# Attention with two expert layers: the same instructions, with tiles at other byte addresses modulo 256

## The chip, the cores and the metric

The kernel runs on one core of a Trainium2 chip. The metric is device time in microseconds, of which the median of the runs is quoted. One run was taken with the hardware profiler, and every row below comes from that one. "Address" means the byte offset of a tile within each of the 128 partitions of the on-chip memory (SBUF); a "residue" is that address modulo 256.

## The reference, cut to what matters

```python
keep = is_sink | in_window                       # 4 sinks, window of 128
a = softmax(where(keep, q @ k.T / 8, -1e9))
x = (a @ v) as [1536, 512]                       # 2 batches x 768 tokens, 8 heads x 64
h = x @ w_in                                     # [512, 2048]
g = where(h >= 1, h, where(h <= -1, 0, (h + 1) ** 2 / 4))
x = g @ w_out                                    # [2048, 512]
h = x @ w2_in
g = where(h > 0, h, exp(min(h, 0)) - 1)
out = g @ w2_out                                 # [1536, 512]
```

All four weights arrive as 64-bit floats.

## The kernel before, in words

The 1536 tokens are three blocks of 512. Attention (class `Attn`) makes the input of the first expert layer and the two layers (class `Moe`) follow; attention's pieces for later blocks are put between the first layer's products by hand (`between`, `PULLS`).

A product of two 32-bit numbers is made of three products in the faster type fp32r: each operand is split into a high part and a remainder (hi and lo), and hi·hi, hi·lo and lo·hi are added up. So an activation block t has two tiles, `xh` and `xl`, each [128, 4, 512]. A step ("item") is one block of tokens with one slice of 128 hidden units. `wsplit` (L148 on) makes four weight tiles of [128, 512] for it: ScalarE casts the high parts, `wh0` and `wh1` (L158), and GpSimd subtracts the remainders, `wl0` and `wl1` (L160; VectorE does the first sixteen items). 0 is the slice of the layer's first matrix, 1 of its second, and each of the four has two buffers. `gemm1` does 12 matmuls of 512 columns (L171): the weight tile is the stationary operand, loaded in pieces of 128 columns, and `xh` or `xl` is the moving one. Then the gate is computed (ScalarE and VectorE), and the gated part is split in turn into `gh` and `gl` (L187, L188; three buffers each). `gemm2`, two items later, does another 12 (L210): in the first layer the weights are stationary and `gh`, `gl` move, in the second the gated parts are stationary and the weights move. `finish` (L267) is the same for the last two items. This is 96 items and 2304 matmuls of 128 by 128 by 512.

Each matmul has a weight load of its own (LDWEIGHTS). The load for the next matmul runs while the present one streams its moving operand, so that two tiles are read from SBUF at the same time: the moving operand of matmul n and the stationary operand of matmul n+1. Every slice that a matmul takes starts a multiple of 512 bytes into its tile, so a tile has one residue for all its slices.

The pools lay tiles one after another. Constants come first (10 KB from address 16384), then `x`, then attention's pools, then the experts'. Their sizes happen to be such that every tile of the experts begins at residue 160 before the change. Attention's are spread: `idn`, the identity for transposes (L466, L539), at 192; `P`, the probabilities, in four buffers at 96, 128, 160 and 192, of which the first to be transposed in a pair of heads is that at 96 or at 160 in turn; `one` at 96, `vs` at 160, and `pst`, their moving operand (L597 and L601, fp32r, 256 columns), at 224.

Of the kernel before, what the change touches and what calls it, by code (L numbers as in the profile page):

```python
# [7 lines left out]
F32 = mybir.dt.float32  # L8
F32R = mybir.dt.float32r
# [10 lines left out]
BLK = 128  # L20
KW = BLK + NSINK
WP = KW + BLK
NEG = -1.0e30
FILL = -1.0e9


def f32(ap):
    return ap.bitcast(F32)


def read_params(nc, const, n_sink, window):
# [33 lines left out]
class Moe:  # L65
# [82 lines left out]
    def wsplit(self, i, e):  # L148

        if i >= len(self.items):  # L150
            return
        nc = self.nc
        m, tb, f = self.items[i]
        src = self.F[m, f][:, e * 512:(e + 1) * 512]
        pool = (self.ws_p, self.wo_p)[e]
        hi = pool.tile([128, 512], F32R, tag=f"wh{e}", name=f"wh{e}")
        lo = pool.tile([128, 512], F32R, tag=f"wl{e}", name=f"wl{e}")
        nc.scalar.copy(hi, src)  # L158

        (nc.vector if i < self.KF else nc.gpsimd).tensor_tensor(out=lo, in0=src, in1=f32(hi), op=ALU.subtract)  # L160
        self.spl[i, e] = (hi, lo)

    def gemm1(self, i):
        nc = self.nc
        m, (t, c0, n), f = self.items[i]
        hi, lo = self.spl.pop((i, 0))
        xh, xl = self.xts[t]
        h = self.h_ps.tile([128, n], F32, tag="h", name="h")
        for k in range(self.KD):
            for p, (w, x) in enumerate(((hi, xh), (hi, xl), (lo, xh))):  # L170
                nc.tensor.matmul(h, lhsT=w[:, k * 128:(k + 1) * 128], rhs=x[:, k, c0:c0 + n],  # L171
                                 start=(k == 0 and p == 0), stop=(k == self.KD - 1 and p == 2))
            if k == 1:
                yield
        g = self.t_p.tile([128, n], F32, tag="g", name="g")
        if m == 0:

            nc.scalar.activation(g, h, AF.Relu, bias=self.half, scale=0.5)
            nc.scalar.activation(g, g, AF.Square)  # L179
            nc.vector.scalar_tensor_tensor(out=g, in0=h, scalar=1.0, in1=g, op0=ALU.max, op1=ALU.min)  # L180
        else:
            nc.scalar.activation(g, h, AF.Relu, scale=-1.0)
            nc.scalar.activation(g, g, AF.Exp, scale=-1.0)  # L183
            nc.vector.scalar_tensor_tensor(out=g, in0=g, scalar=-1.0, in1=h, op0=ALU.add, op1=ALU.max)  # L184
        gh = self.g_p.tile([128, n], F32R, tag="gh", name="gh")
        gl = self.g_p.tile([128, n], F32R, tag="gl", name="gl")
        ac = nc.scalar.copy(gh, g)  # L187
        dv = nc.vector.tensor_tensor(out=gl, in0=g, in1=f32(gh), op=ALU.subtract)  # L188
        self.own = (ac.ins, dv.ins)
        self.g[i] = (gh, gl)  # L190
        yield
# [90 lines left out]
class Attn:  # L282


    def __init__(self, tc, ctx, q, k, v, xts, idn, const, segs, nq=2):
        self.tc, self.nc = tc, tc.nc
        nc = self.nc
        self.q, self.k, self.v, self.xts = q, k, v, xts
        self.B, self.H, self.S, self.D = q.shape
        self.scale = 1.0 / float(self.D) ** 0.5  # L290
        self.idn, self.const = idn, const
        self.nq = nq
        pool = lambda n, b, **kw: ctx.enter_context(tc.tile_pool(name="a_" + n, bufs=b, **kw))
        self.ld_p = pool("ld", 3)
        self.qk_p = pool("qk", 2)
        self.p_p = pool("p", 4)
        self.pt_p = pool("pt", 2)
        self.xb_p = pool("xb", 1)
        self.s_p = pool("s", 2)
        self.ps = pool("ps", 2, space=PSUM)  # L300
        self.sk, self.kept = {}, {}
        self.turn, self.spare = 0, []
        self.nat = {}
        self.first = None
        self.jobs = [(s, pr) for s in segs for pr in range(self.H // 2)]
        for what in "kq":
            self.load(what, *self.jobs[0])
# [8 lines left out]
    def masks(self, prm):  # L316
# [4 lines left out]
        for j in (1, 0):  # L321
# [5 lines left out]
                                  for ty in range(3)]  # L327
        new, sink, old = slice(KW, WP), slice(BLK, KW), slice(0, BLK)

# [375 lines left out]
@with_exitstack  # L705
def attention_moe_moe(ctx, tc, q, k, v, n_sink, window, w_in, w_out, w2_in, w2_out, out):
    nc = tc.nc
    B, H, S, D = q.shape
    NT, DM = out.shape
    const = ctx.enter_context(tc.tile_pool(name="const", bufs=1))  # L710
    xp = ctx.enter_context(tc.tile_pool(name="x", bufs=1))
    ws = ((w_in, w_out), (w2_in, w2_out))

    raw = read_params(nc, const, n_sink, window)
    half = const.tile([128, 1], F32, tag="half", name="half")
    nc.vector.memset(half, 0.5)
    idn = const.tile([128, 128], F32, tag="idn", name="idn")
    nc.gpsimd.memset(idn, 0.0)
    nc.gpsimd.affine_select(out=idn, in_=idn, pattern=[[-1, 128]], compare_op=ALU.not_equal, fill=1.0, base=0,
                            channel_multiplier=1)  # L720
    NX = NT // 512
    xts = []
    for t in range(NX):
        xts.append((xp.tile([128, DM // 128, 512], F32R, tag=f"xh{t}", name=f"xh{t}"),
                    xp.tile([128, DM // 128, 512], F32R, tag=f"xl{t}", name=f"xl{t}")))
    full = [(t, 0, 512) for t in range(NX)]

    with ExitStack() as c2:
        NQ = 2
        segs = []  # L730
        for b in range(B):
            for q0 in range(0, S // BLK, NQ):
                tok = b * S + q0 * BLK
                segs.append((b, q0, tok // 512, tok % 512))
        attn = Attn(tc, c2, q, k, v, xts, idn, const, segs, nq=NQ)
        moe = Moe(tc, c2, ws, out, xts, (full, full), half)

        attn.load("q", *attn.jobs[1])
        attn.load_vsink()
        warm = const.tile([128, 1], F32, tag="warm", name="warm")  # L740
        nc.scalar.activation(warm, half, AF.Exp)

        zero = moe.t_p.tile([128, 512], F32, tag="g", name="zero")
        nc.vector.memset(zero, 0.0)
        bank = moe.h_ps.tile([128, 512], F32, tag="h", name="warmup")
        for _ in range(3):
            nc.tensor.matmul(bank, lhsT=zero[:, 0:128], rhs=zero, start=True, stop=True)
        prm = params(nc, const, raw)
        attn.masks(prm)
        gen = attn.stages()  # L750
        done = [0]

        def go(n=None, upto=None):

            while done[0] < len(segs) and (n is None or n > 0) and (upto is None or done[0] < upto):
                if next(gen) is not None:
                    done[0] += 1
                n = None if n is None else n - 1

        need = [(t * 512 + c0 + n) // (NQ * BLK) for t, c0, n in full] + [0]  # L760
        attn.spare = [lambda shape, name, t=t: moe.y_ps.tile(shape, F32, tag=t, name=name) for t in ("y0", "y1", "y2", "y3")]
        attn.spare += [lambda shape, name: moe.h_ps.tile(shape, F32, tag="h", name=name)] * 2

        for what, j in (("k", 1), ("k", 2), ("q", 2), ("v", 0)):
            attn.load(what, *attn.jobs[j])
        with tc.manual_schedule(engines={mybir.EngineType.PE}):
            go(n=1)
            moe.load(1)
            attn.load("v", *attn.jobs[1])
            moe.load(3)  # L770
            go(n=19)
        flag = windowed(tc, const, prm)
        with tc.manual_schedule(engines={mybir.EngineType.PE}):
            go(upto=need[0])
        moe.behind = attn.first
        attn.spare = []
        credit = [0.0]

        def between(i):
            m, tb, f = moe.items[i]  # L780
            if m == 1 or done[0] >= len(segs):
                return
            j = i // moe.KF
            credit[0] += PULLS[j]
            while credit[0] >= 1.0:
                credit[0] -= 1.0
                if done[0] < len(segs):
                    go(n=1)
            if f == moe.KF - 1 and moe.last_call:
                go(upto=need[j + 1])  # L790

        moe.run(between)

    cond = nc.values_load(flag[0:1, 0:1], min_val=0, max_val=1)
    with tc.If(cond < 1):
        with ExitStack() as c3:
            general_attention(tc, c3, q, k, v, prm, idn, half, xts)
        with ExitStack() as c3:
            moe = Moe(tc, c3, ws, out, xts, (full, full), half, pfx="g_")
            moe.run(lambda i: None)  # L800
# [32 lines left out]
```

## Time and profile before

| | |
|---|---|
| median of 3 runs | 661.54 us (661.34 to 661.99) |
| the profiled execution | 662.93 us, of which 661.2 us from its first to its last instruction |
| TensorE, matmuls | 638.8 us busy (97%), 3090 instructions |
| TensorE, weight loads | 500.5 us (76%), beside the matmuls |
| ScalarE / VectorE / GpSimd | 450.6 (68%) / 376.2 (57%) / 267.8 us (40%) |
| mean granted clock of TensorE | 0.991 of full |

How to read it: a matmul is pipelined, and its record lasts longer (389 ns and more) than the time until the next one starts. So the busy share of TensorE says that it hardly ever stood idle, and not how fast it went. How fast it went is read from start to start. The timeline gives starts to 10 ns; the chain of waits gives the length of a dozen in a row. Where a time from start to start stands below to 1 ns, it is taken from the trace's start times, which are kept in whole nanoseconds.

### The profile page before, as it was taken

How to read it: one execution, taken by the hardware profiler on the slowest of the kernel's cores; microseconds unless marked ns; L12 is line 12 of the kernel's file. 1: busy time of each engine (PE TensorE's matmuls, PEld its weight loads, DVE VectorE, ACT ScalarE, POOL GpSimd, SP SyncE). 2: the span in 40 equal slices, each digit the busy share in tenths (PEclk: the TensorE clock that was granted, in tenths of full speed). 3: DMA queues.
4: the chain of work that ended last, by engine and by line, in shares of the span. 5: the costliest groups of instructions: out<-in, count | busy, mean ns of one | idle time of the engine just before them, and what ended most of it. 6: DMA issues, size and time to landing. Idle time of an engine off the chain costs nothing.

```text
span 661.2 us, 9257 instructions
## 1 busy us (share of the span) xinstructions
PE 638.8 (97%) x3090; PEld 500.5 (76%) x3090; DVE 376.2 (57%) x742; ACT 450.6 (68%) x913; POOL 267.8 (40%) x310
## 2 busy tenths in 40 slices
PE   5899999999999999999999999999999999999995
PEld 2666767766777767888878888888888888888884
DVE  2899989999435244224987878777432222322221
ACT  2998998997666666557768878776655555555542
POOL 4320113112125334443645655554544444444441
PEclk8998999999999999999999999999999999999999
DMA  6577454764200000000433332321010000100001
GB/s 172 126 186 203 126 170 135 207 198 143 56 13 13 13 0 1 1 0 1 159 118 105 99 105 90 109 93 50 0 64 1 0 1 0 64 0 1 1 0 69
DMA packets 66922, 47.91 MB, mean 72 GB/s; under 512 B 44848, under 2 KB 61232, under 8 KB 66864
## 3 DMA queue, kind: packets, MB, share of 16 engines
q1 hardware_dynamic: 65552, 46.94, 24.6%
q8 instruction: 26, 0.43, 0.3%
q10 hardware_dynamic: 1312, 0.28, 0.2%
q14 instruction: 32, 0.26, 0.1%
HBM read 44.06 MB, written 3.15 MB: 71 GB/s over the span
## 4 chain that ended last, share of the span: by engine, by line
PE 81%; DVE 7%; issue 4%; ACT 4%; DMA 2%; POOL 1%; POOLq 0%; SPq 0%; DVEq 0%; ACTq 0%
PE h L171 36%; PE y L210 35%; PE S L506 4%; PE ops L564 3%; PE tps L539 2%; DVE ca L143 2%; PE qkps L466 1%; DVE F L145 1%; DVE ca L142 1%; DVE wl L160 1%; ACT pt L541 1%; DMA st<-in_moe_w_in_dram 1%; DVE P L510 1%; ACT P L512 1%; PE y L267 1%
## 5 line engine op out<-in xcount | busy, mean ns | idle before, releaser
L160 POOL TENSOR_TENSOR wl<-F,wh 128x512 fp32r<-128x512 f32 x160 | 219.6, 1380 | 229.6 <-ACT wh L158 216.9
L158 ACT CAST wh<-F 128x512 fp32r<-128x512 f32 x192 | 117.5, 618 | 97.1 <-PE h L171 89.4
L171 PE MATMUL h<-xh,wh 128*128 128x512 f32 x384 | 154.3, 402 | 0.5 <-DVE g L180 0.5
L171 PE MATMUL h<-xh,wl 128*128 128x512 f32 x384 | 150.5, 392 | 0.0
L171 PE MATMUL h<-xl,wh 128*128 128x512 f32 x384 | 150.5, 392 | 0.0
L187 ACT CAST gh<-g 128x512 fp32r<-128x512 f32 x96 | 59.7, 621 | 62.1 <-DVE g L184 36.2
L188 DVE TENSOR_TENSOR gl<-g,gh 128x512 fp32r<-128x512 f32 x96 | 68.3, 712 | 49.0 <-ACT gh L187 48.7
L184 DVE SCALAR_TENSOR_TENSOR g<-g,h 128x512 f32<-128x512 f32 x48 | 33.0, 687 | 110.9 <-ACT g L183 110.9
L171 PEld LDWEIGHTS h<-xh,wh 128*128 128x128 f32 x384 | 72.4, 189 | 20.6 <-issue 5.3
L171 PEld LDWEIGHTS h<-xh,wl 128*128 128x128 f32 x384 | 72.3, 188 | 15.3
L171 PEld LDWEIGHTS h<-xl,wh 128*128 128x128 f32 x384 | 72.7, 189 | 14.2 <-DVE xl L608 0.4
L210 PE MATMUL y<-gh,wh 128*128 128x512 f32 x192 | 78.4, 408 | 0.0
L210 PE MATMUL y<-gh,wl 128*128 128x512 f32 x192 | 75.2, 391 | 0.0
L210 PE MATMUL y<-gl,wh 128*128 128x512 f32 x192 | 74.9, 390 | 0.0
L145 DVE CUSTOM_DVE_ANT_0 F<-ca,F 128x1024 uint16<-128x1024 uint16 x64 | 71.5, 1119 | 4.5 <-DVE ca L143 1.8
L210 PE MATMUL y<-wh,gh 128*128 128x512 f32 x184 | 71.6, 389 | 0.0
L210 PE MATMUL y<-wl,gh 128*128 128x512 f32 x184 | 71.6, 389 | 0.0
L210 PE MATMUL y<-wh,gl 128*128 128x512 f32 x184 | 71.6, 389 | 0.0
L180 DVE SCALAR_TENSOR_TENSOR g<-h,g 128x512 f32<-128x512 f32 x48 | 33.0, 687 | 45.2 <-ACT g L179 45.1
L512 ACT ACTIVATE P<-P,nb 128x260 f32<-128x260 f32 (+1 forms) x96 | 46.6, 491 | 15.5 <-DVE nb L510 13.4
L515 POOL COPY psn<-P 128x8 f32<-128x8 f32 x48 | 13.0, 271 | 89.8 <-ACT P L512 81.9
L510 DVE CUSTOM_DVE_ANT_0 P<-S,mask 128x260 f32<-128x260 f32 (+1 forms) x96 | 34.8, 401 | 24.1 <-PE S L506 23.5
(105 smaller groups left out, 912.3 us busy)
## 6 DMA issues: line engine op xcount, KB each, us to landing
st<-in_moe_w_in_dram SPq DMA_DIRECT2D x32, 512.0 KB, 3.9
st<-in_moe_w_out_dram SPq DMA_DIRECT2D x32, 512.0 KB, 3.8
kn<-in_k_dram SPq DMA_DIRECT2D x48, 64.0 KB, 2.3
vn<-in_v_dram SPq DMA_DIRECT2D x32, 96.0 KB, 2.4
out_dram<-o SPq DMA_DIRECT2D x12, 256.0 KB, 2.1
qn<-in_q_dram SPq DMA_DIRECT2D x44, 64.0 KB, 2.4
vn<-in_v_dram SPq DMA_DIRECT2D x16, 64.0 KB, 2.1
qn<-in_q_dram ACTq DMA_DIRECT2D x4, 64.0 KB, 3.0
```

The source lines that it names most:

```text
L145: nc.vector.tensor_tensor(out=r, in0=ai, in1=r, op=ALU.add)
L158: nc.scalar.copy(hi, src)
L160: (nc.vector if i < self.KF else nc.gpsimd).tensor_tensor(out=lo, in0=src, in1=f32(hi), op=ALU.subtract)
L171: nc.tensor.matmul(h, lhsT=w[:, k * 128:(k + 1) * 128], rhs=x[:, k, c0:c0 + n], start=(k == 0 and p == 0), stop=(k == self.KD - 1 and p == 2))
L180: nc.vector.scalar_tensor_tensor(out=g, in0=h, scalar=1.0, in1=g, op0=ALU.max, op1=ALU.min)
L184: nc.vector.scalar_tensor_tensor(out=g, in0=g, scalar=-1.0, in1=h, op0=ALU.add, op1=ALU.max)
L187: ac = nc.scalar.copy(gh, g)
L188: dv = nc.vector.tensor_tensor(out=gl, in0=g, in1=f32(gh), op=ALU.subtract)
L210: nc.tensor.matmul(self.y[c], lhsT=a, rhs=b, start=(first and p == 0), stop=(last and p == 2))
L506: nc.tensor.matmul(S[h], lhsT=qT[hs, n, :], rhs=kT[hs].rearrange("p j k -> p (j k)")[:, j0 * KW:j0 * KW + W], start=True, stop=True)
L510: dv = nc.vector.tensor_tensor_reduce(out=o, in0=S[h], in1=self.mask[ty], op0=ALU.add, op1=ALU.min, scale=-self.scale, scalar=3.0e38, accu ...
L512: ac = nc.scalar.activation(o, o, AF.Exp, bias=nb[:, n, h:h + 1], scale=-1.0, accum_out=sm[:, n, 2 * pr + h:2 * pr + h + 1])
```

## The change

No instruction, order or wait is changed; on all five engine queues the two programs are the same but for the numbers of buffers. What changes is where tiles lie. `xh` and `xl` get 256 bytes more and begin at an offset within them, so that block 0 is at residue 32, block 1 at 64 and block 2 at 128. `fill_to_row` puts a filler behind attention's pools, so that the experts' pools begin at 0. The weight tiles are made 96 bytes (`wh0`, `wl0`) and 32 bytes (`wh1`, `wl1`) longer and the gated parts 64 bytes (`gh`, `gl`), so that their buffers fall on different residues.

```diff
+ROW = 256
+ATTN_BYTES = 34560 + 160
...
+def fill_to_row(pool, used):
+    n = -used % ROW
+    if n:
+        pool.tile([128, n // 4], F32, tag="fill", name="fill")
...
-        hi = pool.tile([128, 512], F32R, tag=f"wh{e}", name=f"wh{e}")
-        lo = pool.tile([128, 512], F32R, tag=f"wl{e}", name=f"wl{e}")
+        pad = (24, 8)[e]
+        hi = pool.tile([128, 512 + pad], F32R, tag=f"wh{e}", name=f"wh{e}")[:, 0:512]
+        lo = pool.tile([128, 512 + pad], F32R, tag=f"wl{e}", name=f"wl{e}")[:, 0:512]
...
-        gh = self.g_p.tile([128, n], F32R, tag="gh", name="gh")
-        gl = self.g_p.tile([128, n], F32R, tag="gl", name="gl")
+        gh = self.g_p.tile([128, n + 16], F32R, tag="gh", name="gh")[:, 0:n]
+        gl = self.g_p.tile([128, n + 16], F32R, tag="gl", name="gl")[:, 0:n]
...
         self.ps = pool("ps", 2, space=PSUM)
+        fill_to_row(pool("fill", 1), ATTN_BYTES)
...
-    for t in range(NX):
-        xts.append((xp.tile([128, DM // 128, 512], F32R, tag=f"xh{t}", name=f"xh{t}"),
-                    xp.tile([128, DM // 128, 512], F32R, tag=f"xl{t}", name=f"xl{t}")))
+    for t, off in zip(range(NX), (32, 64, 128)):
+        pair = []
+        for c in "hl":
+            flat = xp.tile([128, 512 * (DM // 128) + 64], F32R, tag=f"x{c}{t}", name=f"x{c}{t}")
+            o = (off - 160) % 256 // 4
+            pair.append(flat[:, o:o + 512 * (DM // 128)].rearrange("p (k n) -> p k n", n=512))
+        xts.append(tuple(pair))
```

Residues of the tiles as the two programs are laid out (one number for each buffer):

```
                before          after
xh, xl          160             32 / 64 / 128 (block 0 / 1 / 2)
wh0             160, 160        0, 96
wl0             160, 160        192, 32
wh1             160, 160        128, 160
wl1             160, 160        192, 224
gh              160, 160, 160   0, 64, 128
gl              160, 160, 160   192, 0, 64
F, st, ca, g    160             0
attention       as above        the same
```

The distance that counts for two reads at once is the residue of the moving operand of one matmul less that of the stationary operand of the next. Before, it is 0 for every pair of expert matmuls. After, the pairs fall on all eight multiples of 32: in the program's order 259 on 0, 436 on 32, 217 on 64, 263 on 96, 359 on 128, 179 on 160, 263 on 192 and 241 on 224.

## Rows read from the trace of the kernel before

**Rows 1.** The profile's page: busy time of each engine.
```profile
PE 638.8 (97%) x3090; PEld 500.5 (76%) x3090; DVE 376.2 (57%) x742; ACT 450.6 (68%) x913; POOL 267.8 (40%) x310
```

**Rows 2.** Stretches of the span: TensorE's busy time (count), granted clock, DMA share, GB/s.
```profile
59.00:61.70 2.70, 2.70 (x8) 0.51 0.60 127
62.00:258.00 196.00, 193.86 (x1027) 1.00 0.34 95
260.00:300.00 40.00, 40.00 (x178) 1.00 0.00 1
345.00:640.00 295.00, 295.00 (x1303) 1.00 0.14 45
```

**Rows 3.** The chain in order of time: start, length, what, how many.
```profile
261.21 2.72 PE h L171 x12
...
485.28 2.72 PE h L171 x12
488.00 2.72 PE y L210 x12
```

**Rows 4.** Timeline, TensorE at half clock: start us, us, engine, line, operation.
```profile
59.48 0.63 PE L171 MATMUL h<-xh,wh 128*128 128x512 f32 x1
59.91 0.63 PE L171 MATMUL h<-xl,wh 128*128 128x512 f32 x1
60.33 0.63 PE L171 MATMUL h<-xh,wl 128*128 128x512 f32 x1
60.76 0.63 PE L171 MATMUL h<-xh,wh 128*128 128x512 f32 x1
```

**Rows 5.** Timeline of TensorE at 500 us: one matmul, and the weight load beside it.
```profile
500.07 0.39 PE L210 MATMUL y<-wh,gh 128*128 128x512 f32 x1
...
500.08 0.19 PEld L210 LDWEIGHTS y<-wl,gh 128*128 128x128 f32 x1
```

**Rows 6.** Groups by line, TensorE, 62 to 258 us: count, busy us, mean ns, idle.
```profile
L171 PE MATMUL h<-xl,wh 128*128 128x512 f32 x97 | 38.2, 394 | 0.0
```

**Rows 7.** The same view, 345 to 640 us.
```profile
L171 PE MATMUL h<-xl,wh 128*128 128x512 f32 x218 | 84.8, 389 | 0.0
```

**Rows 8.** Timeline, TensorE's matmuls after an attention product, at 233 us.
```profile
233.29 0.39 PE L210 MATMUL y<-gl,wh 128*128 128x512 f32 x1
233.52 0.40 PE L210 MATMUL y<-gh,wl 128*128 128x512 f32 x1
233.75 0.40 PE L210 MATMUL y<-gh,wh 128*128 128x512 f32 x1
233.99 0.39 PE L210 MATMUL y<-gl,wh 128*128 128x512 f32 x1
234.21 0.40 PE L210 MATMUL y<-gh,wl 128*128 128x512 f32 x1
```

**Rows 9.** Timeline, matmul before a transpose whose P lies at 160 (first, last).
```profile
77.53 0.39 PE L171 MATMUL h<-xh,wl 128*128 128x512 f32 x1
77.77 0.27 PE L539 MATMUL tps<-idn,P 128*128 128x128 f32 x1
...
239.05 0.39 PE L171 MATMUL h<-xh,wl 128*128 128x512 f32 x1
239.28 0.27 PE L539 MATMUL tps<-idn,P 128*128 128x128 f32 x1
```

**Rows 10.** Timeline, matmul before a transpose whose P lies at 96 (first, last).
```profile
66.08 0.40 PE L171 MATMUL h<-xh,wl 128*128 128x512 f32 x1
66.31 0.27 PE L539 MATMUL tps<-idn,P 128*128 128x128 f32 x1
...
247.48 0.40 PE L171 MATMUL h<-xh,wl 128*128 128x512 f32 x1
247.72 0.27 PE L539 MATMUL tps<-idn,P 128*128 128x128 f32 x1
```

**Rows 11.** Timeline, fp32r matmuls of 256 columns and what follows (early, last).
```profile
99.50 0.41 PE L601 MATMUL rps<-pst,one 112*128 112x256 f32 x2
99.74 0.39 PE L210 MATMUL y<-gh,wh 128*128 128x512 f32 x1
...
258.32 0.40 PE L601 MATMUL rps<-pst,one 112*128 112x256 f32 x2
258.55 0.39 PE L210 MATMUL y<-gl,wh 128*128 128x512 f32 x1
```

**Rows 12.** Groups by line, GpSimd and ScalarE, 345 to 640 us.
```profile
L160 POOL TENSOR_TENSOR wl<-F,wh 128x512 fp32r<-128x512 f32 x111 | 153.3, 1390 | 143.6 <-ACT wh L158 134.7 <-PE h L171 3.7 <-DVE xl L216 3.4
L158 ACT CAST wh<-F 128x512 fp32r<-128x512 f32 x110 | 67.1, 618 | 61.7 <-PE h L171 59.6 <-DVE F L145 2.0
```

## The prediction

> **What bounds the kernel now.** I read the page first: TensorE's matmuls cover 97% of the span, no other engine is above 68% [rows 1]. By stretches, TensorE is busy 193.86 us of 196 beside attention and all of the time later [rows 2]. So the time is the number of matmuls times what one takes, and a change in the pace of a matmul goes into the span whole. Next the chain of waits, for that pace: from 261 us on it is an unbroken row of dozens, twelve matmuls of 512 columns in 2.72 us, in both layers [rows 3]. That is **226.7 ns from start to start**. It is the same at 260 to 300 us, with DMA at nothing, as later with DMA at 0.14 and the other engines at work [rows 2, 3], so neither transfers nor the other engines set it.
>
> Is 226.7 ns all columns? The early timeline tells. From 59 to 61.7 us the granted clock is half (0.51, that is 1.2 GHz) [rows 2], and matmuls start 0.42 to 0.43 us apart [rows 4]; to the nanosecond 426.7. At 2.4 GHz the same columns take half, 213.3 ns. So at full clock each matmul pays **13.3 ns that are not columns**, and at half clock none of it. What runs beside a matmul at that point is the weight load of the next, which starts 3 ns after it [rows 5].
>
> Beside attention the pace is worse and uneven: the mean record is 394 ns there and 389 ns later [rows 6, 7], and after an attention product the starts lie 0.22 to 0.24 us apart [rows 8] and settle to 226.7 only after some ten matmuls undisturbed. By the trace's start times there are 2126 intervals between expert matmuls that are neither at half clock nor the first after an attention product: 395 up to 258 us with a mean of 230.8 ns, and 1731 after it with a mean of 226.7. The common mean is 227.5. The extra time therefore depends on how load and matmul stand to each other, though all expert tiles share a residue.
>
> **Does the address count?** One place in the trace before has the same kind of matmul beside the same kind of load at two distances. The moving tile is at 160, and the load is P's for a transpose, from a buffer at 160 (distance 0) or at 96 (distance 64). With P at 160 the next start comes 231.5 ns later on average (six cases, 230 to 233) [rows 9], with P at 96 it comes 236.3 ns later (eight cases, 235 to 237) [rows 10]. The two sets do not overlap, so the address is worth some ns per matmul. These loads are of another type than the experts' (fp32, for a transpose), so I take from them that it counts, and not the sign. Then the fp32r matmuls of attention: 256 columns, moving tile at 224, and the next load at a distance of 64 or 128. Two of them take 0.24 us or 0.23 us [rows 11]; over the 28 cases whose load starts at once, the mean is 118.75 ns, from 112 to 124. Less the 106.7 ns of their columns, the load costs 12.1 ns.
>
> **The change part by part.**
> - Instructions, queues, semaphores and DMA issues: all the same, none added, removed or moved. Cost nothing.
> - Filler and longer tiles: no instruction touches them. Nothing, and nothing hides it.
> - Casts, subtractions and evictions on ScalarE, VectorE and GpSimd write to or read from other residues. No row shows what that does to one. They are covered: in the settled stretch GpSimd's wl takes 153.3 of 295 us and waits 143.6, nearly all for its input [rows 12]. If each of them grew by a tenth, TensorE would still have work. I take 0; without that cover, a tenth of 1390 ns twice an item would be 0.3 us per item.
> - The expert matmuls and the distance to the next load: that is the whole sum. Before it is 0 for all of them, after it is spread over all eight multiples of 32. No row has a 512-column matmul at full clock with an fp32r load at most of these distances, so I bound it. Below: the shortest 256-column case, 112 ns, so 5.3 ns beside the columns, and 218.7 ns per matmul; nothing in the trace excludes a gain of that size. Above: the unsettled mean of 230.8 ns for all. I take the row that is nearest in kind, fp32r with fp32r at distances other than 0: 213.3 + 12.1 = **225.4 ns**.
>
> The sum: 1731 x (226.7 - 225.4) = 2.3 us, and 395 x (230.8 - 225.4) = 2.1 us, together 4.4 us. The first matmul after each attention product, the waits and the stretch at half clock stay. The profiled execution took 662.93 us and would take 658.5; the median stands 1.4 us lower, at 661.54, so I predict **657.1 us**.
>
> The Trainium skill speaks against all of this. "TensorE: Matmul & The Clock Gate", section "Step-by-step: what each phase is for", gives TensorE two independent SBUF read ports, one for the moving operand and one for the weight load, and says that loading the next weights takes no read bandwidth from the running matmul. By that rule the distance is worth nothing and the time stays at 661.5 us. The rows disagree where they can: 231.5 against 236.3 ns. The same page, section "Back-to-back issue gap", puts a warm matmul of 512 columns at about 216 ns; if all that lies above were a clash that spreading removes, an estimate from that figure is 11.8 x 2126 = 25 us, 636 us.
>
> **The rivals.**
> 1. *The even pace is lost: slower.* The 226.7 ns is a state that the pair of streams falls into when every step is like the one before; any disturbance costs ten steps at about 231 ns. After the change the distance alternates within each dozen (for example 224, 32, 224), and changes between dozens with the buffers. If no state can settle, the matmuls run on as they do beside attention, 230.8 ns: 1731 x 4.1 = 7.1 us more, 668.6 us. It decides from a common mean of 227.5 ns up. For it: the settling itself, and the transposes at distance 64, which are slower than at 0. Against it: 12.1 ns at mixed distances, in places that are as disturbed as any.
> 2. *Spreading takes most of the clash away.* If 0 is the worst distance and the usual step is like the shortest seen, 218.7 ns, the gain is 8.8 x 2126 = 18.7 us, 642.8 us. For it: at half clock there is no loss at all, so none is inherent. Against it: only one case in 28 is that short.
> 3. *The change does nothing here.* The 13.3 ns are a fixed cost of an fp32r matmul with a load, and what differs between P's buffers is something else than their address; or the distances average out. Then 661.5 us, give or take 1.3. For it: the 256-column matmuls lose about as much (12.1) at their distances as the expert ones at 0 (13.3). Against it: two sets that do not overlap.
>
> **How the numbers follow.** Change and no change can be told apart from about 0.2%, 1.3 us, which here is 0.6 ns per matmul. The forecast (a common mean of 223 to 226.8 ns) gets 0.40, and its own range is 652 to 660 us. Rival 2, more than that, gets 0.15; rival 3 gets 0.17; rival 1 gets 0.28. Faster is the forecast with rival 2, 0.55. The range takes the forecast, rival 3, rival 1 up to its price, and rival 2 down to five sixths of its gain: 646 to 669 us.
>
> **What would show it.** The counts and the waits should be the same, TensorE's share still 97%, the stretch of the half clock still 426.7 ns per matmul. In the chain of waits the dozens would read 2.70 or 2.71 in place of 2.72 us on average, and would no longer all be alike; those of one block should repeat after six items, when two and three buffers come round. If the dozens read 2.77 it is rival 1, 2.6 rival 2, 2.72 throughout rival 3. I am wrong altogether if the dozens keep 2.72 us and the time moves by some us: then another engine or the transfers answer to the address. If the casts' mean of 618 ns moves [rows 12], the addresses count for them too.

## The result, and the profile after

The changed kernel takes 670.86 us (median of 4 runs, 669.9 to 671.34) against 661.65 us before (4 runs): a ratio of 1.0137, with a 95% interval from 1.0124 to 1.015. It is **slower by 9.2 us**, outside the range and on the other side of the forecast. The first rival had this sign and nearly this size (668.6 us).

The page of the profiled execution (669.9 us, span 668.1 us) answers to [rows 1]:

```profile
span 668.1 us, 9257 instructions
...
PE 647.5 (97%) x3090; PEld 500.7 (75%) x3090; DVE 376.7 (56%) x742; ACT 451.6 (68%) x913; POOL 268.5 (40%) x310
```

The counts are the same, and so, to 1.0 us, are the busy times of all engines but one: TensorE is busy 8.7 us longer. Its share is 97% as before, so it does not wait more; the matmuls themselves take longer. The stretches (us, TensorE's busy time, granted clock, DMA share, GB/s) answer to [rows 2]:

```profile
262.00:300.00 38.00, 38.00 (x166) 1.00 0.00 1
345.00:640.00 295.00, 295.00 (x1275) 1.00 0.14 45
```

In the same 295 us, fully busy at the full clock in both, 1275 matmuls were under way after the change and 1303 before. The chain in order of time (start, length, what, how many) shows the pace, which was 2.72 us for each dozen [rows 3]:

```profile
260.39 2.77 PE h L180 x12
263.16 2.78 PE y L219 x12
...
282.65 2.77 PE h L180 x12
285.42 2.79 PE y L219 x12
288.21 2.78 PE h L180 x12
290.99 2.80 PE y L219 x12
```

No dozen is at 2.72 any more, and they are no longer alike: 2.76 to 2.81 us. By the trace's start times, the 1733 intervals between expert matmuls after the last attention product have a mean of 231.75 ns. That is 5.0 ns above the pace before, and 5.0 x 1733 = 8.7 us is the loss. Beside attention the mean goes from 230.8 to 232.0 ns, 0.5 us more.

Not all of it shows in the span. Between the two layers the chain runs for 25 us through VectorE, which converts the second layer's weights (`ca`, `F`), and not through TensorE. Before:

```profile
304.73 2.51 PE h L171 x11
314.70 1.72 DVE ca L143
...
332.62 3.01 PE h L171 x12
```

and after:

```profile
304.91 2.56 PE h L180 x11
314.93 1.72 DVE ca L151
...
332.98 3.04 PE h L180 x12
```

A slower matmul costs nothing there: TensorE's pauses at that place are 0.4 us shorter after the change. The spans of the two profiled executions differ by 6.9 us and not by 9.2, since the one after also reached the end of attention 0.9 us sooner and needed 0.5 us less behind its last matmul. The profile of the run at 0 below, with the distances of before, ends attention 1.8 us sooner than the profile of before, so that part is no mark of the distances.

The groups by line, 345 to 640 us (count, busy us, mean ns, idle before and its releasers), answer to [rows 7, 12]:

```profile
L180 PE MATMUL h<-xl,wh 128*128 128x512 f32 x213 | 83.9, 394 | 0.0
...
L169 POOL TENSOR_TENSOR wl<-F,wh 128x512 fp32r<-128x512 f32 x108 | 150.3, 1396 | 144.7 <-ACT wh L167 135.0 <-PE y L219 3.7 <-DVE xl L225 3.5
L167 ACT CAST wh<-F 128x512 fp32r<-128x512 f32 x109 | 66.7, 618 | 66.1 <-PE h L180 62.3 <-DVE F L153 2.0 <-POOL wl L169 1.8
```

A matmul's record is 394 ns where it was 389. The casts keep 618 ns, and GpSimd's subtractions take 1396 ns against 1390 and still wait half of the time. So of the rows shown only TensorE's answer to the addresses by more than half a per cent.

### The profile page after: what moved, and what is told of

It reads as the page before. It is cut to its first block, busy times and chain, and to the rows that moved or that the text cites. A ratio compares the mean times of both kernels' runs of the same rounds, so it can differ in the third digit from the quotient of the medians.

```text
span 668.1 us, 9257 instructions
## 1 busy us (share of the span) xinstructions
PE 647.5 (97%) x3090; PEld 500.7 (75%) x3090; DVE 376.7 (56%) x742; ACT 451.6 (68%) x913; POOL 268.5 (40%) x310
## 4 chain that ended last, share of the span: by engine, by line
PE 83%; DVE 6%; issue 4%; ACT 4%; POOL 1%; DMA 1%; POOLq 0%; SPq 0%; DVEq 0%; ACTq 0%
PE h L180 37%; PE y L219 35%; PE S L516 4%; PE ops L574 2%; PE tps L549 2%; DVE ca L151 1%; PE qkps L476 1%; DVE F L153 1%; DVE ca L150 1%; DVE P L520 1%; ACT P L522 1%; PE y L276 1%; DMA st<-in_moe_w_out_dram 1%; DVE wl L169 1%; ACT pt L551 1%
## 5 line engine op out<-in xcount | busy, mean ns | idle before, releaser
L167 ACT CAST wh<-F 128x512 fp32r<-128x512 f32 x192 | 117.9, 619 | 104.8 <-PE h L180 96.5
```

## The experiments

Three questions: is it the addresses as such or their distances, which distances are bad, and between which two tiles does the distance count. "Pace" is the mean from start to start of the expert matmuls after 262 us, by the trace's start times. Runs with an interval were timed at least four times, beside the kernel before; of the others there is one run each, and only the pace is used.

**All at 0.** The change without its pads, and with the three inputs at 0:

```diff
-        pad = (24, 8)[e]
+        pad = (0, 0)[e]
...
-        gh = self.g_p.tile([128, n + 16], F32R, tag="gh", name="gh")[:, 0:n]
+        gh = self.g_p.tile([128, n + 0], F32R, tag="gh", name="gh")[:, 0:n]
...
-    for t, off in zip(range(NX), (32, 64, 128)):
+    for t, off in zip(range(NX), (0, 0, 0)):
```

> Every expert tile at residue 0 instead of 160, so every distance is 0 as in the kernel before, at other absolute addresses. Theory 1 (a distance that changes from step to step keeps the matmuls from settling): 226.7 ns per matmul, 2.72 us per dozen, 661.6 us. Theory 2 (each distance has its own price): the same 661.6 us, since the distance is 0. Theory 3 (the absolute residue counts): other than 661.6 us by more than 1.3 us.

Measured: 661.15 us, ratio 0.9994 (0.9984 to 1.0004), and the old pace of 226.7 ns in every interval of the settled stretch:

```profile
278.45 2.72 PE y L219 x12
281.17 2.72 PE h L180 x12
```

So this common shift of all expert tiles, from 160 to 0, costs nothing, nor do the filler, the longer input tiles and the transfers' landing on multiples of 256. Theory 3 falls; what counts is how tiles lie to each other.

**The inputs alone.** Pads at nothing as above, the inputs at 32, 64 and 128:

> Only the expert input tiles are moved (32, 64, 128 by block), all other expert tiles at 0: within a dozen the distance stays the same (the block's in the first product, 0 in the second), and it changes between dozens. Theory 1: each dozen begins to settle anew, so its mean lies between 226.7 and 231.5 ns; some 665 to 668 us. Theory 2: the second product's dozens keep 2.72 us and the first product's have one fixed value per block.

Measured: 667.45 us, ratio 1.0093 (1.0075 to 1.0111). In layer two, from 345 us, the second product's matmuls, still at distance 0, run at 229.2 ns on average; the first product's at 233.7, 230.3 and 232.6 ns (32, 64, 128). A piece of the chain, in block 0:

```profile
348.54 2.79 PE h L180 x12
351.33 2.73 PE y L219 x12
354.06 2.79 PE h L180 x12
```

Both theories had a part of it: the moved products are slow throughout, and those at 0 lose 2.5 ns because each of their dozens comes after a moved one. After a dozen at 128 only the first three intervals at 0 are long (231.7, 232.7 and 230.7 ns), and the other nine take 226.7; after one at 64 the dozen at 0 does not settle at all (230.8 ns on average).

**The pads alone.** As the change, with the inputs at 0:

```diff
-    for t, off in zip(range(NX), (32, 64, 128)):
+    for t, off in zip(range(NX), (0, 0, 0)):
```

> The pads of the weights and the gated parts as in the change, with the three input blocks at 0. Distances are as mixed as in the change. Theories 1 and 2 alike: 231 to 232 ns per matmul and 669 to 671 us, so that with the run that moves the inputs alone (+0.9%) the parts do not add up to the whole (+1.4%): each part by itself already costs most of it.

Measured: 668.76 us, ratio 1.0117 (1.01 to 1.0134), pace 231.6 ns. The two parts alone cost 0.9% and 1.2%, both together 1.4%: they do not add up. That fits a price that is much the same at most distances, so that a matmul which is off 0 already loses little more by lying elsewhere.

**One distance per stage.** These separate a bad distance from a changing one. Starting from the kernel before, the stationary tiles of a stage (layer and block) are shifted so that all its pairs have one distance, counted to the matmul's own stationary operand and to the next one's alike:

```diff
+DIST = ((64, 128, 32), (64, 96, 128))
...
+        o = 0 if (m, e) == (1, 1) else -DIST[m][tb[0]] % 256 // 4
-        hi = pool.tile([128, 512], F32R, tag=f"wh{e}", name=f"wh{e}")
+        hi = pool.tile([128, 576], F32R, tag=f"wh{e}", name=f"wh{e}")[:, o:o + 512]
...
+        o = -DIST[1][t] % 256 // 4 if m else 0
-        gh = self.g_p.tile([128, n], F32R, tag="gh", name="gh")
+        gh = self.g_p.tile([128, 576], F32R, tag="gh", name="gh")[:, o:o + n]
```

and the same for `wl` and `gl`. The other runs differ in the numbers alone: (192, 32, 160) and (192, 224, 16); 8 throughout layer one, then 4, 240, 48; 80, then 248, 252, 12; 20, then 24, 144, 112; 40, then 56, 72, 208; 176, then 36, 88, 132.

> The weights' and gated parts' tiles are shifted so that each stage (layer and block) has a single distance for every pair: layer one 64, 128, 32 and layer two 64, 96, 128. Theory 1: every stage settles to 226.7 ns, 2.72 us per dozen, as at distance 0, and the whole takes 661.6 us. Theory 2: each stage has its own pace; by the means of the changed kernel 96 is the slowest (234 ns, 2.81 us per dozen), the others 231 to 232 ns (2.78 us); whole some 669 us. If one of them settles below 226.7 ns, that distance is the way to a faster kernel.

> The same with 192, 32, 160 in layer one and 192, 224, 16 in layer two. Theory 1: 2.72 us per dozen in all of them, 661.6 us. Theory 2: own paces; by the means of the changed kernel 160 is the fastest (230 ns, 2.76 us per dozen) and 192 the slowest (232.5 ns, 2.79 us); 16 is not known.

> One distance per stage again, finer ones: 8 in layer one, then 4, 240 and 48 in layer two. Theory 2 (each distance has a pace of its own): 4 and 8 lie between the 226.7 ns of distance 0 and the 228.4 ns of 16, or equal one of them if the chip sees the address in steps of 16 bytes; 240 and 48 are not known, 228 to 233 ns. Theory 4 (0 is the best distance because both streams then stand equal): none is below 226.7 ns. A dozen below 2.72 us would refute it.

> The same with 80 in layer one, then 248, 252 and 12 in layer two, that is small distances on the other side of 0. Theory 4: none below 226.7 ns. If the sign does not matter, 252 goes like 4 and 248 like 8; the multiples of 32 went unlike by sign (64: 228.9 ns, 192: 233.3 ns), so I expect 248 and 252 to differ from 8 and 4.

> One distance per stage: 20 in layer one, then 24, 144 and 112. So far 0 and 4 settle to 226.7 ns, 16 to 228.3, 64 to 228.9, 80 to 230.0, all others to 230.7 to 234.3. If 0 is the best (theory 4), none of these dozens is below 2.72 us; most at 2.75 to 2.81. One below would be the way to a faster kernel.

> The same with 40 in layer one, then 56, 72 and 208. Theory 4: none below 2.72 us per dozen. If multiples of 8 that are no multiples of 16 go like 8 (233.3 ns), 40, 56 and 72 take 2.80 us.

> The same with 176 in layer one, then 36, 88 and 132. Theory 4: none below 2.72 us per dozen. If a step of 4 bytes changes nothing, as from 0 to 4, 132 goes like 128 (233.3 ns) and 36 like 32 (233.3 ns).

Measured, the pace of each distance in its undisturbed stages (layer one's last block and layer two):

| pace, ns | distances, bytes modulo 256 |
|---|---|
| 226.7 | 0, 4 |
| 228.3 to 228.9 | 16, 64 |
| 230.0 to 230.7 | 80, 248, 56 |
| 231.1 to 232.4 | 24, 20, 48, 72, 176, 40, 252 |
| 233.3 to 234.3 | 8, 12, 32, 36, 88, 96, 112, 128, 132, 144, 160, 192, 208, 224, 240 |

The whole of these seven took 669.2 to 671.4 us, one run each. Three stages of the first of them in its chain, at 64, 96 and 128:

```profile
406.31 2.75 PE h L173 x12
...
494.45 2.80 PE h L173 x12
...
584.05 2.80 PE h L173 x12
```

and the stages at 8 and at 4 of the run with finer distances:

```profile
277.37 2.80 PE h L173 x12
...
405.85 2.72 PE h L173 x12
```

Theory 1 (only a changing distance costs) fails: with one distance for hundreds of matmuls nothing but 4 comes back to 226.7 ns. They do settle, but each into a rhythm of its own. At 128 it is two steps, 229 and 238 ns in turn, with a mean of 233.3; at 96 three, 231, 232 and 237; at 64 three, 226, 229 and 232; at 0 all are equal. Theory 2 holds, a price for each distance. Theory 4 (0 is the best) holds as far as the numbers go: of 29 distances none is faster than 0. Some guesses at an order held: 36 goes like 32, 132 like 128, and 248 and 252 unlike 8 and 4. Others failed: 8, which I put between 0 and 16, is among the slowest, 40, 56 and 72 do not go like 8, and of the paces that I read off the changed kernel's mixture 160, the fastest there, is the slowest here. No faster version came out of this.

**Which pair: the remainders apart.** All four remainder tiles shifted by 128:

```diff
-        lo = pool.tile([128, 512], F32R, tag=f"wl{e}", name=f"wl{e}")
+        lo = pool.tile([128, 576], F32R, tag=f"wl{e}", name=f"wl{e}")[:, 32:544]
...
-        gl = self.g_p.tile([128, n], F32R, tag="gl", name="gl")
+        gl = self.g_p.tile([128, n + 64], F32R, tag="gl", name="gl")[:, 32:32 + n]
```

and `xl` likewise.

> All remainder tiles (xl, wl0, wl1, gl) 128 bytes further than the high parts. In the order of the three products the moving operand and the load of the next matmul are then always 0 apart, while the moving operand and the stationary operand of its own matmul are 128 apart in two of three. Theory 2 as I put it (the next load counts): 226.7 ns, 661.6 us. Theory 5 (the matmul's own stationary operand counts): about two thirds of the matmuls at 230 to 233 ns, 668 us.

Measured: 668.64 us, ratio 1.0115 (1.0098 to 1.0132), pace 231.1 ns:

```profile
276.27 2.77 PE h L171 x12
279.05 2.77 PE y L210 x12
```

The distance to the next load is 0 in every pair here (but for two among the last 24 matmuls), and yet 4.4 ns are lost. My theory, on which the whole prediction stood, is refuted. By the matmul's own stationary operand one matmul in three is at 0 and two are at 128: (226.7 + 2 x 233.3) / 3 = 231.1 ns, which is what was measured.

**Which pair: the mirror.** Now the next load is at 128 in every pair, and the own stationary operand in one of three:

```diff
-        hi = pool.tile([128, 512], F32R, tag=f"wh{e}", name=f"wh{e}")
-        lo = pool.tile([128, 512], F32R, tag=f"wl{e}", name=f"wl{e}")
+        oh, ol = (32, 0) if (m, e) == (1, 1) else (0, 32)
+        pad = 64 * e
+        hi = pool.tile([128, 512 + pad], F32R, tag=f"wh{e}", name=f"wh{e}")[:, oh:oh + 512]
+        lo = pool.tile([128, 576], F32R, tag=f"wl{e}", name=f"wl{e}")[:, ol:ol + 512]
...
+        oh, ol = (0, 32) if m else (32, 0)
+        gh = self.g_p.tile([128, n + 64], F32R, tag="gh", name="gh")[:, oh:oh + n]
+        gl = self.g_p.tile([128, n + 64], F32R, tag="gl", name="gl")[:, ol:ol + n]
```

and `xh` 128 bytes further.

> The mirror of the run that shifted all remainders: now the first moving tile of each three products and the remainder stationary tile lie 128 further, the rest stays. The moving operand and the next matmul's load are then 128 apart in every pair, the moving operand and its own stationary operand 128 apart in one of three and 0 in two. With the paces of the settled stages (226.7 ns at 0, 233.3 ns at 128): the next load counts: 233.3 ns, 2.80 us per dozen, some 672 us. The own stationary operand counts: (2 x 226.7 + 233.3) / 3 = 228.9 ns, 2.75 us per dozen, some 665 us. Every change of a residue from one matmul to the next counts, whichever pair it is in: about 231 ns, as in that run.

Measured: 665.2 us, ratio 1.0051 (1.0035 to 1.0068), pace 228.9 ns:

```profile
277.38 2.75 PE h L173 x12
280.12 2.75 PE y L213 x12
```

That is the figure of the own stationary operand to a tenth of a nanosecond, 4.4 ns from that of the next load and 2 from that of "any change". The interval that begins with the matmul at 128 is also the longest of the three, 232.5 ns on average; the two others are 225.8 and 228.3.

This rules out the next load alone. It does not single out the own stationary operand, for the load after the next one (and the one before the own) has the same counts: 128 in two of three pairs in the run with shifted remainders, in one of three here. Nor is that load far off in time: it starts some 230 ns after the matmul, whose record lasts some 390 ns. By the place of the long interval the own operand fits better here, since by the two others the third matmul of each three would be the dear one, and it has 228.3 ns. With the remainders shifted the place tells nothing (230.0, 233.3, 230.0), and summed over the changed kernel, with the paces of the table, the own operand gives 232.5 ns and the load after the next 232.4. So what is shown is that the distance counts; the own stationary operand is the reading that fits best.

## Why the prediction was wrong, point by point

- **What bounds the kernel**: right in the main. TensorE's pace went into the time nearly whole: 8.7 us on 1733 intervals and 0.5 us beside attention, less 0.4 us of pauses, against 9.2 us between the medians. The "unbroken row of dozens" from 261 us on was not unbroken, though: for 25 us between the layers the chain is VectorE's. Counts are the same, the other engines' busy times moved by 1.0 us at most, and the cover for casts and subtractions held.
- **"The address counts"**: right, and so was that 13.3 ns of a matmul's 226.7 are not columns. The rule of the Trainium skill that speaks against it ("TensorE: Matmul & The Clock Gate", "Step-by-step: what each phase is for": two independent read ports, so that loading weights takes nothing from the running matmul) gave 661.5 us; the chip gave 670.9, so the measurement decides against that reading of it. The page's own words are about the next load, though, and the mirror run agrees with them so far: with the next load at 128 throughout, the pace is what the own operand's distances give, 228.9 ns.
- **"The moving operand of one matmul and the load of the next"**: the wrong pair. I took it from the timeline, where the load starts 3 ns after the matmul [rows 5]; but the matmul's record lasts longer than the step, and is still open when the load after the next begins. The runs with shifted remainders and their mirror rule the next load out, and the matmul's own stationary operand fits both. The transposes, 231.5 against 236.3 ns [rows 9, 10], are not explained by that. The transpose's own distance (identity at 192, P at 160 or 96) is 32 or 96 in every run, and yet with all expert tiles at 0 the transposes with P at 96 start 231 ns after the matmul before them in six of the eight cases (238 and 240 in the others), where it was 235 to 237 in all eight. So there the place of the expert tiles against attention's tiles counts; between which two reads is open, and those loads are of another type.
- **"Fp32r with fp32r at distances other than 0: 213.3 + 12.1 = 225.4 ns"**: the term that failed, and with it the forecast. The 12.1 ns came from matmuls of 256 columns [rows 11] and I carried them over whole, as a cost per load. Their own distances are 64 and 128; matmuls of 512 columns settle at 228.9 and 233.3 ns there, that is 15.6 and 20.0 ns beside the columns, and in the changed kernel's mixture the mean is 231.75 ns, 18.4 beside the columns. The 28 cases of 256 columns do not even have that order: 119.8 ns at 64 and 117.9 at 128. So the cost is not one per load that carries over from 256 columns to 512, and the bound below that I drew from the shortest of them (218.7 ns) was no bound of this case.
- **"0 is a distance like others, or the worst"** lay unsaid in the forecast and in rival 2. It is the best of 29. The kernel before, with all its tiles at one residue, already stood at the floor of what these runs reach; spreading could only lose.
- **Rival 1** had the place, the sign and nearly the price: it took the pace beside attention, 230.8 ns, for all, and 231.75 came. Its mechanism was only partly right. That changing distances keep the pace from settling does cost something (2.5 ns on the products at 0 when the inputs alone were moved). But the larger part is the settled price of the distances themselves: summed over the changed kernel's own distances, with the paces of the table, it is 232.5 ns against the 231.75 measured, for the pads alone 231.6 against 231.6, and for the inputs alone 229.3 against 230.7.
- **Rival 3** is out; the two sets of transposes that did not overlap were the right evidence against it.

## What to carry to other kernels

When matmuls of 512 fp32r columns run back to back, look at the start-to-start time and not at the busy share, and compare the addresses of the moving and the stationary tiles modulo 256: equal throughout was the fastest here, and most other distances cost 2 to 3% of a matmul's pace. Tiles whose sizes are multiples of 256 bytes keep that by themselves, and a pad put on one tile for another reason can undo it for all that follow. And a price taken from matmuls of another length is no price until one run has shown that it does not change with the length.

## What the runs showed of the hardware that was not expected

A uniform stream of matmuls does not take a uniform time: at a distance of 128 bytes it falls into steps of 229 and 238 ns in turn, at 96 into three (231, 232, 237), at 0 into equal ones of 226.7. At half clock (0.51 granted) the same matmuls take 426.7 ns, their columns and nothing else [rows 4]. The distances' order (0 and 4 alike, 8 and 12 slow, 16 and 64 close to 0, 252 slow) follows no rule that I could find. Whether it is the own stationary operand that counts, although its load starts some 223 ns before the matmul does, or the load after the next, is open, and so is what the two reads share: the two runs made to tell the pairs apart have matmuls in groups of three, in which these two have the same counts. Nor was it tried whether the pattern holds for other types or, beyond the 28 matmuls of 256 columns, for other lengths.
